# Attention beside a two-dimensional Fourier filter: the filter's steps regrouped into threes, its product copied out of the bank, a weight split moved to VectorE

## The chip, the cores and the metric

The kernel runs on one core of a Trainium2 chip. The metric is the device time of one execution in microseconds. The engines named here are TensorE (PE in the profile, its weight loads PEld), VectorE (DVE), ScalarE (ACT), GpSimd (POOL) and SyncE (SP), which only issues DMA transfers.

## The reference

Two independent halves are computed and put side by side. The first is attention with 16 query heads and one shared key and value head; the second is a filter in the frequency domain.

```python
# S, D, H, Dh = 2048, 448, 16, 28
q = (x @ wq) split into 16 heads;  k = x @ wk;  v = x @ wv
scores = einsum("bhqd,bkd->bhqk", q, k) * Dh ** -0.5
a = (softmax(scores) @ v, heads joined) @ wo

X = rfft2(xB)                       # (2048, 448) -> (2048, 225)
y = irfft2(X * (w_r + 1j * w_i))
out = concatenate([a, y], axis=-1)
```

All inputs and outputs are float32.

## The kernel before

A first part projects the queries, keys and values, prepares the keys and does the first stage of the Fourier transform (the lines up to 450). After it comes one long loop, in which the change lies.

The loop runs over 16 pairs (c, g): four chunks c of 512 queries and four groups g of four heads. For each pair it makes 16 steps, one for each 128 keys, so there are 256 steps. A step makes four score matmuls (L719), one for each head, into four PSUM banks; ScalarE takes the exponential of each (L720) into SBUF tiles p. The value products of a step (L699, eight records in the profile) follow later: `flush` issues them for all steps of the batch before, at the end of a batch. A batch is an entry of `PLAN`, a list of steps that share one such change from scores to value products and back. A step's entry names the units that it also carries. The units are small pieces of the other work: F ends the first transform; A (`fft2_a`, 16 of them) multiplies two columns by the matrix g1 in three matmuls (L484 to L486) and then by the filter on VectorE; B (`fft2_b`, 16) multiplies by g2; Z (32) is the third stage, in turn `fft3_a` and `fft3_b`, two of each for each of eight parts; W (48) is the output projection.

PAIR is two steps with no unit, THERE three steps with B in the first and A in the second, OUT three steps with two W, BACK three steps with one Z. A unit in the first step comes after that step's third score, in a later step after its fourth.

Each score and each unit takes a PSUM bank from the head of a queue, `take()`. A score's bank goes to the tail at once, a unit's bank comes back by `give(bank, n)` n scores later. There are six banks s, and the banks sx and po join them; one bank at a time holds the output being summed, so seven go round. Whoever takes a bank waits until it has been read. The orders of TensorE and VectorE are exactly those in which the program writes them; those of the other queues are set by a scheduler that keeps the dependences.

On VectorE a unit A means: the multiplies with the filter's real and imaginary part (L525 to L527, which read the bank), their sum (L528), a rounding to the matmul format (L530) and the remainder (L532); then `fft2_split` for the next A (L514, L515). A unit B means a copy of its bank to cst (L543), and each second B is followed by a store of cst to a scratch tensor t2 in DRAM (L546). At the end of a pair (c, g) its output bank is copied to osb (L707), and four `norm` calls per pair (five operations each, L606 to L613) divide it by the softmax sums; the rule `has_time(step)` says which steps may carry one. Each pair's fifth step builds the next pair's queries (`build_q`, L189 to L191 on VectorE, then nine transfers on SyncE).

`fft2_load` fetches the inputs of two A's, b on SyncE and wr and wi on GpSimd's queue. `fft3_load` fetches the inputs of four Z's: c from t2 on SyncE (L561) and constants on GpSimd's queue. The first of them needs all of t2, which means all 16 B. `wo_split` fetches a group of the output weights and splits it into a rounded part and a remainder, for the W units: a transfer and two operations on GpSimd (L478 to L480), in steps 20, 28, 36 and 44.

Of the kernel before, what the change touches and what calls it, by code (L numbers as in the profile page):

```python
# [10 lines left out]
F32 = mybir.dt.float32  # L11
# [4 lines left out]
ALU = mybir.AluOpType  # L16
# [4 lines left out]
S, D, H = 2048, 448, 16  # L21
DH = D // H
DF = D // 2 + 1
# [9 lines left out]
P_BUFS = 12  # L33


PAIR, OUT, BACK, THERE = ["", ""], ["W", "W", ""], ["Z", "", ""], ["B", "A", ""]
PLAN = ([["F"], [""]] + 4 * [PAIR] + 2 * [["A", ""]] + 6 * [THERE, THERE, PAIR] + 2 * [THERE] + 2 * [["B", ""]]
        + 8 * [OUT] + 10 * [BACK] + [PAIR]
        + 3 * [BACK] + 8 * [OUT] + 9 * [BACK] + 2 * [PAIR]
        + 3 * [BACK] + 8 * [OUT] + 7 * [BACK] + 5 * [PAIR])  # L40
TAIL = 0
WARM = 10, 10

# [2 lines left out]
def kernel(ctx: ExitStack, tc: tile.TileContext, t: dict):  # L46
    nc = tc.nc
# [4 lines left out]
    fp = ctx.enter_context(tc.tile_pool(name="fp", bufs=2))  # L52
# [15 lines left out]
    def behind(ins, other):  # L68

        tc.add_manual_dep(ins.ins, other.ins.name,  # L70
                          mybir.DependencyInfo(mybir.DependencyClass.NoSync, mybir.DependencyReason.DATA),
                          reason="order of issue")
# [136 lines left out]
    with tc.tile_pool(name="w1", bufs=1) as w1, tc.tile_pool(name="p1", bufs=6, space=PSUM) as p1:  # L209
# [37 lines left out]
        with tc.tile_pool(name="x1", bufs=2) as x1:  # L247
# [18 lines left out]
            xr, wr = {}, {}  # L266
# [192 lines left out]
    def give(bank, scores=1):  # L459

        late.append([scores, bank])
# [7 lines left out]
    ap = ctx.enter_context(tc.tile_pool(name="ap", bufs=2))  # L469
    pp = ctx.enter_context(tc.tile_pool(name="pp", bufs=P_BUFS))  # L470

    begun = []
    woh = ap.tile([128, NG, D], F32R, name="woh", bufs=1)
    wol = ap.tile([128, NG, D], F32R, name="wol", bufs=1)

    def wo_split(g):
        w = ap.tile([128, D], F32, name="wo", tag="ya")
        behind(nc.gpsimd.dma_start(w, t["wo"][:, g]), begun[-1])  # L478
        nc.gpsimd.tensor_copy(woh[:, g], w)
        nc.gpsimd.tensor_tensor(wol[:, g], w, woh[:, g].bitcast(F32), op=ALU.subtract)  # L480


    def mm3(out, w, h, l):
        mm(out, fc[w + "h"], h, start=True, stop=False)  # L484
        mm(out, fc[w + "l"], h, start=False, stop=False)  # L485
        mm(out, fc[w + "h"], l, start=False, stop=True)  # L486
# [20 lines left out]
    def halves2(bank):  # L507
        return bank[:, :2 * DF].rearrange("p (n f) -> p n f", n=2)
# [8 lines left out]
    def fft2_a(u):  # L517
        q, v = divmod(u, 2)
        s = slice(2 * v, 2 * v + 2)
        b, wr, wi = (b2[n, q][:, s] for n in ("b", "wr", "wi"))  # L520
        bank = take()
        pu = halves2(bank)
        mm3(pu, "g1", b2["h", u], b)
        pf, p2 = fp.tile([128, 2, DF], F32, name="pwr"), fp.tile([128, 2, DF], F32, name="pwi")
        nc.vector.tensor_tensor(pf, pu, wr, op=ALU.mult)  # L525
        nc.vector.tensor_tensor(p2[0:64], pu[64:128], wi[64:128], op=ALU.mult)
        nc.vector.tensor_tensor(p2[64:128], pu[0:64], wi[0:64], op=ALU.mult)  # L527
        nc.vector.scalar_tensor_tensor(pf, p2, sgn, pf, op0=ALU.mult, op1=ALU.add)  # L528
        h = fp.tile([128, 2, DF], F32R, name="ph")
        nc.vector.tensor_copy(h, pf)  # L530
        p = fp.tile([128, 2, DF], F32R, name="pl")
        nc.vector.tensor_tensor(p, pf, h.bitcast(F32), op=ALU.subtract)  # L532
        pr[u] = h, p
        give(bank, 2)

    def fft2_b(u):
        v = u % 2
# [107 lines left out]
    def at(step, f, *a):  # L645
        later.setdefault(max(step, 0), []).append((f, a))

    todo = {"F": [(fft1_b, 7)],
            "A": [(fft2_a, u) for u in range(16)],
            "B": [(fft2_b, u) for u in range(16)],  # L650
            "W": [(wo_unit, c, k, g) for c in range(NC - 1) for k in range(4) for g in range(NG)],
# [3 lines left out]
    place, where = [], {}  # L655
    for b, batch in enumerate(PLAN):
        for i, kinds in enumerate(batch):
# [10 lines left out]
        if u % 2 == 0 and u < 14:  # L668
            at(step - 1, fft2_load, u // 2 + 1)
    for g in range(NG):  # L670
        at(20 + 8 * g, wo_split, g)
    for q in range(8):
        at(max(where["Z"][4 * q] - 8, where["B"][-1] + 1), fft3_load, q)

# [1 line left out]
    norms = deque()  # L676

    def has_time(step):
        b, i, _ = place[step]
        if step % 16 == 4:  # L680
            return False
        if PLAN[b] is THERE:
            return i == 0 and len(norms) > 4
        return i < 2

    def waits_for_output(c):
        return where["W"][16 * c - 1] if c else -1
# [5 lines left out]
    def flush(b, last=False):  # L693
        while pend and pend[0][0] < b:
            _, c, g, kc, ps = pend.pop(0)
            if kc == 0:
                po[c, g] = take() if po else ps_o.tile([128, 512], F32, name="po")
            for i in range(4):
                mm(po[c, g][32 * i:32 * i + 32], vs[:, kc], ps[i // 2][:, i % 2], start=(kc == 0), stop=(kc == 15))  # L699
            if kc == 15:  # L700
                o = osb[c, g] = ap.tile([128, CW], F32, name="osb")
                if last:
                    for k in range(4):
                        s = slice(128 * k, 128 * k + 128)
                        nc.scalar.activation(o[:, s], po[c, g][:, s], AF.Copy)
                else:
                    nc.vector.tensor_copy(o, po[c, g])  # L707
                    give(po[c, g])
                    norms.extend((c, g, k) for k in range(4))

    for c, g in order:
        for kc in range(16):
            ps = []
            b, i, kinds = place[step]
            for n in range(4):
                if n % 2 == 0:
                    ps.append(pp.tile([128, 2, CW], F32, name="p"))
                sc = take()
                begun.append(mm(sc, ka[:, kc * 128:(kc + 1) * 128], qa[c, g][:, n], start=True, stop=True))  # L719
                nc.scalar.activation(ps[-1][:, n % 2], sc, AF.Exp, scale=SCALE)  # L720
                scored(sc)

                if n == (3 if i else 2):
                    for k in kinds:
                        f, *a = todo[k].popleft()
                        f(*a)
            if i + 1 == len(PLAN[b]):
                flush(b)
            if step == 1:
                give(ps_x.tile([128, 512], F32, name="sx", tag="aux"))  # L730
            pend.append((b, c, g, kc, ps))
            for f, a in later.pop(step, []):
                f(*a)
            if norms and has_time(step) and step > waits_for_output(norms[0][0]):
                norm(*norms.popleft())
            if kc == 4 and step < 240:
                build_q(*order[step // 16 + 1])
            step += 1
# [8 lines left out]
    def partial(k):  # L747
        ws.append(take()[:, :D])
        wo_mm(ws[k], c, k, range(NG - 1))

    for k in range(TAIL):
        partial(k)
    flush(len(PLAN), True)
    for k in range(TAIL, 4):
# [125 lines left out]
```

## Time and profile before

| | us |
|---|---|
| three runs | 658.11, 659.64, 659.93 (median 659.64) |
| the profiled execution | 657.37 |
| its span | 655.6 |
| TensorE busy in the span | 649.4 |
| ScalarE busy | 556.0 |
| VectorE busy | 348.9 |
| GpSimd busy | 63.3 |

The span runs from the first to the last instruction of the profiled execution. The granted TensorE clock is 1.000 throughout. The busy times are shares of one span and overlap; a busy matmul is one that has begun and is modelled not to have ended. In rows of a timeline the first number is the start and the second the length, both in microseconds, and "x16" says that 16 instructions were merged into the row. In rows of groups the last numbers are the total busy time in microseconds and the mean of one instruction in nanoseconds. In rows of DMA issues stand the size of one transfer and the median time from its issue to its landing.

The first score of the loop starts at 70.17, step 10 at 89.64. In the plan before, the A units lie in steps 10 to 66, the B units in 14 to 70, the W units in 72 to 94, 137 to 159 and 201 to 223, the Z units in 96 to 134, 161 to 198 and 225 to 243.

### The profile page before, as it was taken

Reading aid. Unit: us, or ns where it says so; the run is one execution under the profiler, and the core shown is the slowest. Engines: PE = TensorE matmul, PEld = TensorE weight load, DVE = VectorE, ACT = ScalarE, POOL = GpSimd, SP = SyncE. Lnnn points to the kernel's source line nnn. Section 1 sums busy time; section 2 is a strip of 40 time slices with the busy share of each in tenths; the row PEclk is TensorE's granted clock in tenths of the full one; section 3 lists DMA queues with packets and bytes.
Section 4 is the critical chain, followed back from the end, with each engine's and each line's share of the span. In section 5 each row is a group of like instructions: output and inputs, shape, how many; then the busy total and the mean of one; then the engine's idle time right before and its main releaser. Section 6 shows DMA issues by size and latency. Waiting matters only on the chain.

```text
span 655.6 us, 11894 instructions
## 1 busy us (share of the span) xinstructions
PE 649.4 (99%) x4480; PEld 376.5 (57%) x4480; DVE 348.9 (53%) x785; ACT 556.0 (85%) x1103; POOL 63.3 (10%) x113
## 2 busy tenths in 40 slices
PE   9999999999999999999999999999999999999997
PEld 6877545555555555565655555655555565555545
DVE  6999448778888851047371701057452502076603
ACT  5554998998888898899998988899999988899992
POOL 3022203212110000001010000000101000010100
PEclk9999999999999999999999999999999999999999
DMA  8756766736352251204141311114150303112001
GB/s 301 255 155 169 197 170 165 183 93 174 101 150 73 70 138 32 63 20 120 41 110 29 94 31 46 47 43 110 44 123 15 96 14 90 32 40 55 29 0 57
DMA packets 34250, 61.86 MB, mean 94 GB/s; under 512 B 6529, under 2 KB 22802, under 8 KB 33228
## 3 DMA queue, kind: packets, MB, share of 16 engines
q1 hardware_dynamic: 30544, 49.18, 27.1%
q0 software_dynamic: 3072, 11.00, 6.6%
q8 instruction: 36, 0.59, 0.4%
q10 hardware_dynamic: 576, 0.92, 0.4%
q14 instruction: 22, 0.18, 0.1%
HBM read 29.35 MB, written 14.75 MB: 67 GB/s over the span
## 4 chain that ended last, share of the span: by engine, by line
PE 88%; DVE 1%; ACT 0%; ACTq 0%; issue 0%; DVEq 0%
PE s L719 29%; PE s L699 29%; PE po L719 5%; PE sx L719 5%; PE sx L699 4%; PE s L619 4%; PE po L699 2%; PE s L582 2%; PE s L570 1%; PE po L619 1%; PE s L486 1%; PE s L484 1%; PE s L485 1%; PE sx L570 0%; ACT yb L624 0%; PE sx L619 0%
## 5 line engine op out<-in xcount | busy, mean ns | idle before, releaser
L720 ACT ACTIVATE p<-s 128x512 f32<-128x512 f32 x759 | 414.9, 653 | 45.1 <-PE s L719 44.3
L719 PE MATMUL s<-qa,ka 128*128 128x512 f32 x759 | 242.4, 408 | 0.6 <-ACT vs L448 0.6
L699 PE MATMUL s<-p,vs 128*32 128x512 f32 x1664 | 194.2, 596 | 0.0
L719 PEld LDWEIGHTS s<-qa,ka 128*128 128x128 f32 x759 | 137.5, 188 | 87.7 <-ACT p L720 62.8
L699 PEld LDWEIGHTS s<-p,vs 128*32 128x32 f32 x1664 | 46.6, 109 | 107.1 <-issue 103.5
L720 ACT ACTIVATE p<-sx 128x512 f32<-128x512 f32 x129 | 84.4, 654 | 6.9 <-PE sx L719 6.8
L720 ACT ACTIVATE p<-po 128x512 f32<-128x512 f32 x136 | 87.1, 641 | 3.4 <-PE po L719 3.2
L607 DVE RECIPROCAL r<-r 128x128 f32<-128x128 f32 x64 | 61.0, 953 | 2.2
L626 DVE COPY ya<-s 128x448 f32<-128x448 f32 x10 | 6.2, 625 | 101.3 <-PE s L619 101.3
L719 PE MATMUL po<-qa,ka 128*128 128x512 f32 x136 | 55.4, 407 | 0.0
L719 PE MATMUL sx<-qa,ka 128*128 128x512 f32 x129 | 52.7, 408 | 0.0
L590 POOL TENSOR_TENSOR yo<-y 128x226 f32<-128x226 f32 x16 | 9.7, 606 | 376.5 <-issue 287.9
L584 DVE COPY m<-s 128x452 f32<-128x452 f32 x13 | 8.2, 629 | 45.9 <-PE s L582 44.8
L719 PEld LDWEIGHTS sx<-qa,ka 128*128 128x128 f32 x129 | 24.2, 188 | 14.1 <-ACT p L720 9.5
L719 PEld LDWEIGHTS po<-qa,ka 128*128 128x128 f32 x136 | 25.6, 188 | 9.2 <-ACT p L720 5.0
L699 PE MATMUL sx<-p,vs 128*32 128x512 f32 x256 | 30.1, 596 | 0.0
L302 PE MATMUL pq<-xh,wqh 128*128 128x512 f32 x64 | 25.7, 401 | 0.0
L302 PE MATMUL pq<-xh,wql 128*128 128x512 f32 x64 | 25.3, 395 | 0.2
L306 ACT ACTIVATE qraw<-pq 128x512 f32<-128x512 f32 x16 | 9.2, 600 | 17.5 <-PE pq L302 17.5
L608 DVE TENSOR_TENSOR osb<-osb,r 128x128 f32<-128x128 f32 x64 | 18.8, 293 | 2.2
L606 DVE STREAM_SHUFFLE r<-osb 128x128 f32<-128x128 f32 x64 | 19.0, 297 | 0.0
L572 DVE COPY z<-s 113x512 f32<-113x512 f32 (+1 forms) x11 | 7.6, 691 | 21.3 <-PE s L570 21.3
(190 smaller groups left out, 698.5 us busy)
## 6 DMA issues: line engine op xcount, KB each, us to landing
qa<-qa SPq DMA_DIRECT2D x15, 512.0 KB, 4.3
raw<-xa SPq DMA_DIRECT2D x16, 256.0 KB, 4.8
xb<-xb SPq DMA_DIRECT2D x8, 512.0 KB, 3.6
qa<-qh SPq DMA_DIRECT2D x60, 64.0 KB, 2.0
qa<-ql SPq DMA_DIRECT2D x60, 64.0 KB, 2.0
ob<-yo SPq DMA_DIRECT2D x16, 226.0 KB, 2.2
t<-bs SPq DMA_DIRECT2D x16, 225.0 KB, 4.4
wr<-wr POOLq DMA_DIRECT2D x16, 225.0 KB, 4.8
```

The costliest lines, as they stand in the source:

```text
L302: mm(pq, w[:, j, gs], x[:, j], start=(j == 0 and n == 0), stop=(j == 3 and n == 1))
L306: nc.scalar.activation(qraw[:, g, cs], pq, AF.Copy)
L582: mm(py[:, k], z[:w, r, js], cs3[:w, k], start=True, stop=True)
L584: nc.vector.tensor_copy(m, py)
L590: nc.gpsimd.tensor_tensor(yo[:, 0:2], y1[:, 0], y1[:, 1], op=ALU.add)
L606: nc.vector.stream_shuffle(r, o, [DH] * 32)
L607: nc.vector.reciprocal(r, r)
L608: nc.vector.tensor_tensor(o, o, r, op=ALU.mult)
L619: mm(p, x[c][:, g, s], w[:, g], start=(g == 0 and n == 0), stop=(g == NG - 1 and n == 2))
L699: mm(po[c, g][32 * i:32 * i + 32], vs[:, kc], ps[i // 2][:, i % 2], start=(kc == 0), stop=(kc == 15))
L719: begun.append(mm(sc, ka[:, kc * 128:(kc + 1) * 128], qa[c, g][:, n], start=True, stop=True))
L720: nc.scalar.activation(ps[-1][:, n % 2], sc, AF.Exp, scale=SCALE)
```

## The change

Five things change in the loop.

1. The plan. In place of pairs and of threes with two units the Filter stage has two batches A, six batches BOTH (the same as THERE) and then A and B in turn, each in a batch of three with one unit. The last two A and three B come after the first eight OUT. All pairs are gone but the four at the start, and there are 88 batches instead of 94. The A units now lie in steps 10 to 67, 97 and 103, the B units in 16 to 70, 100, 106 and 109; the Z units start at 112. The rest has the same order.
2. In `fft2_a` VectorE first copies the bank to an SBUF tile us, and the multiplies read us. The bank is given back one score later instead of two.
3. `wo_split` is parted: the transfer stays on GpSimd's queue, six steps ahead, in steps 28, 34, 40 and 46; the rounding and the remainder are made on VectorE in steps 34, 40, 46 and 52, after the cst copy of a B.
4. `has_time` now says: the first two steps of any batch without an A, except each pair's fifth step. In the Filter stage the norms so start at step 34 instead of 21.
5. By the same formula as before, the first `fft3_load` now stands at step 110, as the last B is at 109; before it stood at 88.

```diff
-PAIR, OUT, BACK, THERE = ["", ""], ["W", "W", ""], ["Z", "", ""], ["B", "A", ""]
-PLAN = ([["F"], [""]] + 4 * [PAIR] + 2 * [["A", ""]] + 6 * [THERE, THERE, PAIR] + 2 * [THERE] + 2 * [["B", ""]]
-        + 8 * [OUT] + 10 * [BACK] + [PAIR]
-        + 3 * [BACK] + 8 * [OUT] + 9 * [BACK] + 2 * [PAIR]
-        + 3 * [BACK] + 8 * [OUT] + 7 * [BACK] + 5 * [PAIR])
+PAIR, OUT, BACK = ["", ""], ["W", "W", ""], ["Z", "", ""]
+A, B, BOTH = ["A", "", ""], ["B", "", ""], ["B", "A", ""]
+PLAN = ([["F"], [""]] + 4 * [PAIR] + 2 * [A] + 6 * [BOTH] + [B] + 6 * [A, B] + 8 * [OUT] + 2 * [A, B] + [B]
+        + 9 * [BACK] + 8 * [OUT] + 13 * [BACK] + 8 * [OUT] + 10 * [BACK])
...
+    def wo_load(g):
+        wo[g] = ap.tile([128, D], F32, name="wo", tag="ya")
+        behind(nc.gpsimd.dma_start(wo[g], t["wo"][:, g]), begun[-1])
+
     def wo_split(g):
-        w = ap.tile([128, D], F32, name="wo", tag="ya")
-        behind(nc.gpsimd.dma_start(w, t["wo"][:, g]), begun[-1])
-        nc.gpsimd.tensor_copy(woh[:, g], w)
-        nc.gpsimd.tensor_tensor(wol[:, g], w, woh[:, g].bitcast(F32), op=ALU.subtract)
+        nc.vector.tensor_copy(woh[:, g], wo[g])
+        nc.vector.tensor_tensor(wol[:, g], wo[g], woh[:, g].bitcast(F32), op=ALU.subtract)
...
         mm3(pu, "g1", b2["h", u], b)
+        us = fp.tile([128, 2, DF], F32, name="us", bufs=1)
+        nc.vector.tensor_copy(us, pu)
+        give(bank)
         pf, p2 = fp.tile([128, 2, DF], F32, name="pwr"), fp.tile([128, 2, DF], F32, name="pwi")
-        nc.vector.tensor_tensor(pf, pu, wr, op=ALU.mult)
-        nc.vector.tensor_tensor(p2[0:64], pu[64:128], wi[64:128], op=ALU.mult)
-        nc.vector.tensor_tensor(p2[64:128], pu[0:64], wi[0:64], op=ALU.mult)
+        nc.vector.tensor_tensor(pf, us, wr, op=ALU.mult)
+        nc.vector.tensor_tensor(p2[0:64], us[64:128], wi[64:128], op=ALU.mult)
+        nc.vector.tensor_tensor(p2[64:128], us[0:64], wi[0:64], op=ALU.mult)
...
-        give(bank, 2)
...
     for g in range(NG):
-        at(20 + 8 * g, wo_split, g)
+        at(where["B"][g + 6] - 6, wo_load, g)
+        at(where["B"][g + 6], wo_split, g)
...
-        if PLAN[b] is THERE:
-            return i == 0 and len(norms) > 4
-        return i < 2
+        return i < 2 and "A" not in PLAN[b]
```

More of the change, by code (lines that the diff above doesn't have):

```diff
@@ L474 @@
     wol = ap.tile([128, NG, D], F32R, name="wol", bufs=1)
+    wo = {}
+    def wo_load(g):
+        wo[g] = ap.tile([128, D], F32, name="wo", tag="ya")
+        behind(nc.gpsimd.dma_start(wo[g], t["wo"][:, g]), begun[-1])
     def wo_split(g):
-        w = ap.tile([128, D], F32, name="wo", tag="ya")
-        behind(nc.gpsimd.dma_start(w, t["wo"][:, g]), begun[-1])
-        nc.gpsimd.tensor_copy(woh[:, g], w)
-        nc.gpsimd.tensor_tensor(wol[:, g], w, woh[:, g].bitcast(F32), op=ALU.subtract)
+        nc.vector.tensor_copy(woh[:, g], wo[g])
+        nc.vector.tensor_tensor(wol[:, g], wo[g], woh[:, g].bitcast(F32), op=ALU.subtract)
     def mm3(out, w, h, l):
```

## The prediction

> **What bounds the kernel now.** I read the page first, then the busy time by windows, the timelines of the three engines that matter, the chain of waits, the waits of the weight loads and the DMA issues.
>
> ```profile
> PE 649.4 (99%) x4480; PEld 376.5 (57%) x4480; DVE 348.9 (53%) x785; ACT 556.0 (85%) x1103; POOL 63.3 (10%) x113
> ```
> ```profile
> 89.60:230.60 141.00, 140.71 (x844) 75.91 (x840) 116.63 (x234) 125.17 (x251) 22.68 (x38) 1.00 0.49 128
> ```
>
> TensorE has no room left. The second line is a window, with the share of each engine in turn: the Filter stage, steps 10 to 71; VectorE is busy 116.63 of 141.00 us, the fullest stretch it has, and ScalarE 125.17, that is 2.02 us a step or 6.06 for three. A busy TensorE may still be waiting, since the ends of matmuls are modelled; so I count starts, here in the five plain pairs at the end:
>
> ```profile
> 629.54 1.92 PE L699 MATMUL s<-p,vs 128*32 128x512 f32 x16
> ...
> 632.44 0.39 PE L719 MATMUL sx<-qa,ka 128*128 128x512 f32 x1
> 632.67 0.86 PE L719 MATMUL s<-qa,ka 128*128 128x512 f32 x3
> 633.47 1.92 PE L699 MATMUL s<-p,vs 128*32 128x512 f32 x16
> ```
>
> Scores start 0.233 us apart (632.44 to 632.67, and 0.86 less 0.39 over two). The second fence comes from the chain:
>
> ```profile
> 97.80 1.85 PE po L699 x16
> ...
> 103.87 1.85 PE po L699 x16
> ...
> 110.39 1.85 PE po L699 x16
> ...
> 115.32 2.71 PE s L699 x24
> ...
> 205.04 2.71 PE s L699 x24
> ```
>
> Sixteen value products take 1.85 and twenty-four 2.71, so a step's eight cost 0.86. A plain pair lasts 3.93 (629.54 to 633.47); less 8 x 0.233 and 2 x 0.86 that leaves 0.35, paid once a batch for going from scores to value products and back. From 97.80 to 103.87 lies a batch of three with two units that empties a pair: 6.07 = 1.72 + 2.80 + 0.35 + two units, so a unit is 0.6. This builds every batch: three steps with one unit after three steps 2.80 + 2.58 + 0.35 + 0.6 = 6.33, with two units 6.93, both above ScalarE's 6.06. TensorE stays the bound, and only two things move the end: the number of batches, and waits in which TensorE stands still.
>
> **What is taken away.** The plan goes from 94 batches to 88 with the same scores, value products and units: 6 x 0.35 = 2.1 us off.
>
> The old waits of the Filter stage go too. The batch from 103.87 has the same make as the one before and lasts 6.52: 0.45 lost. From 110.39 to 115.32 is 4.93 where the build gives 4.79: 0.15. From 115.32 to 205.04 lie five rounds of two threes with two units and a pair, 89.72; one round builds to 17.78, so 0.8 is lost. The waits of the weight loads name one more:
>
> ```profile
> PEld sx L484 <- DVE bh L514: 0.7, 1, 0.7
> ```
>
> That is the second unit A, at step 12; with the other half of its operand behind it I put 0.8. Together 2.2 us, which I take off whole and put back below where they return. The output weights' split leaves GpSimd; its four loads of them stay on GpSimd's queue, two batches ahead of their use, behind loads of wr and wi whose buffers are free by then. Those two batches, 12.7 us, hide them; if the queue held them up longer, VectorE would stand at the split and the copies behind it would be late.
>
> **What is added: VectorE's work and its order.** TensorE waits when VectorE reads a product's bank too late. Seven banks go round. A unit in the first step (after three scores) has its product about 1.6 us after the batch's first score, and its bank is asked for again at the last step's third score: 0.1 + 10 x 0.233 + 0.6 = 3.0 us. In a batch with two units it is the second score, 3.4 us. VectorE's prices:
>
> ```profile
> 121.42 0.63 DVE L525 TENSOR_TENSOR pwr<-s,wr 128x450 f32<-128x450 f32 x1 [1.14 <-PE s L486]
> ...
> 126.05 0.62 DVE L543 COPY cst<-s 128x450 f32<-128x450 f32 x1
> ```
> ```profile
> 222.84 0.54 DVE L189 TENSOR_SCALAR qt<-qraw,mask,cvec 128x512 f32<-128x512 f32 x1
> ...
> 224.49 0.01 DVE L606 LOAD_MASK_SELECT r<-osb  x1
> ...
> 228.31 0.01 DVE L606 LOAD_MASK_SELECT r<-osb  x1
> ...
> 230.43 0.01 DVE L606 LOAD_MASK_SELECT r<-osb  x1
> ```
> ```profile
> L515 DVE TENSOR_TENSOR b<-b,bh 128x450 fp32r<-128x450 f32 x16 | 10.0, 628 | 0.6
> ...
> L707 DVE COPY osb<-s 128x512 f32<-128x512 f32 x12 | 8.3, 689 | 18.2 <-PE s L699 18.2
> L526 DVE TENSOR_TENSOR pwi<-s,wi 64x450 f32<-64x450 f32 x13 | 8.2, 629 | 0.4
> ```
>
> A unit A with the next split takes 4.63 (121.42 to 126.05), building queries 1.65 (222.84 to 224.49), a norm 2.12 (228.31 to 230.43), a product's copy 0.62 (L543), an eviction of an output bank about 0.6. The new copy is the cst copy by shape and source, with its start 0.66; its bounds are nothing and the 0.69 of L707. The multiplies then read SBUF: two inputs from SBUF cost 628 ns (L515), one from PSUM 629 (L526), so nothing is gained there, and A becomes 5.29. [...] A group of output weights costs VectorE a subtraction of 0.63 (L515) and a cast between nothing and 0.69; I take 1.0.
>
> With these, place by place:
> - Second A, now at step 13: TensorE comes 0.94 later (a step more in the batch before), its operand 0.66 later, so of the 0.8 stay 0.4.
> - Step 20: the eviction of the first output bank meets a batch with two units, 0.2, as it did in pairs.
> - Steps 20 to 24: with t from the first score of step 19, the product of A at 20 is there at 3.5, VectorE is done at 8.8, builds queries until 10.4 and only then copies B's product of step 22, until 11.05. That bank is asked for at 6.93 + 0.1 + 3.4 = 10.4: 0.6, and 0.1 for restarting the weight load. 0.7.
> - Steps 34 to 39: with t from step 34, VectorE comes free from A at 32 at 1.8; cst to 2.4, output weights to 3.4, two norms to 7.6, eviction 8.2, queries 9.8, and the copy for A at 37 ends at 10.5. Its bank is asked for at 6.33 + 3.0 = 9.3. 1.3 with the restart.
> - Steps 226 to 231: a copy and two sums, two norms, eviction, queries, then the copy of the next product at about 10.4; asked for at 9.9. 0.5. Before, the norms fell on 225, 226 and 229, with one less ahead of this copy.
> - The pairs of batches from 40 to 67: 0.6 + 1.0 + 2 x 2.12 from 1.6 ends at 7.4, the next A's product comes at 7.9. Hidden, with half a microsecond and the 0.8 that the bank allows.
>
> **What is added: the third transform right behind the second.** Before, the last B was at step 70 and the first Z at 96. Now they stand at 109 and 112, one batch apart. SyncE's issues before:
>
> ```profile
> 229.51 0.53 SPq L546 DMA_DIRECT2D t<-cst  x1
> 230.98 0.50 SPq L201 DMA_DIRECT2D qa<-qa  x1
> 232.23 2.80 SPq L561 DMA_DIRECT2D c<-t  x4
> 240.79 0.36 SPq L628 DMA_DIRECT2D oa<-ya  x1
> 241.20 1.87 SPq L561 DMA_DIRECT2D c<-t  x4
> ```
> ```profile
> t<-bs SPq DMA_DIRECT2D x16, 225.0 KB, 4.4
> ...
> c<-t SPq DMA_DIRECT2D x32, 112.5 KB, 2.5
> ```
>
> The first load waits for the last store, 229.51 to 232.23 = 2.72; four loads take 1.87 to issue, the last begins after three quarters of it, 1.40; a load lands after 2.5. With t from step 109: product 1.6, copy to 2.3, store, first load 5.0, last load 6.4, landed 8.9. The first Z wants it at 6.33 + 0.8 = 7.1. TensorE stands for 1.9 with the restart, and behind it in its order all scores, so ScalarE too. Behind the waiting loads on SyncE stand the next loads of this kind and the queries of step 116, due at 128; they have time. On GpSimd the Z's constants are fetched well ahead. The bounds: 1.2 if the store lands in the 2.5 of a load and the four issues take half a microsecond less, and 4.5 if the issue is the slow one above (2.80 for 1.87) and the store takes the 4.4 of the first transform's stores (first line of the last fence).
>
> **The sum.** 0.4 + 0.2 + 0.7 + 1.3 + 0.5 + 1.9 = 5.0 added, 2.1 + 2.2 = 4.3 taken away: 0.7 slower. The profiled execution took 657.37 (span 655.6 and 1.8 around it), so 658.1; that execution lies 2.27 below the median of the runs, 659.64, and against the median the forecast is 660.3. About 0.3%, 2 us, is what a measurement of this kernel can tell from no change.
>
> **The rivals.**
> - The third transform's load is later than I have it, slower: all four transfers, the store ahead of them and the wait of TensorE lie in one chain, and each microsecond there is a microsecond of the end. A wait of 4.1 instead of 1.9 gives 662.5; it decides from a wait of 3.3 on. For it: the slow issue and the 4.4 us stores. Against: at 230.98 the slow one shared its queue with a transfer of queries that is not there at step 110. Chance 0.15.
> - VectorE's backlog grows, slower: if its operations in this stage come out 6% longer, each chain of eight to ten microseconds ahead of a bank is half a microsecond longer, in four places, and an eviction joins them: about 2.4 more than the forecast, 662.7; it decides from 1.3 on. For it: 116.63 of 141.00 already, and no plain pairs left to catch up in. Against: the work is spread over 48 more steps, and GpSimd's arithmetic beside it is gone. Chance 0.17.
> - The new waits hardly come, faster: VectorE runs further ahead than I have it and the load lands sooner, as in its lower bound. With 1.5 left of 5.0 the end is 656.8. For it: each of the four waits is the small difference of two long sums. Against: two have over a microsecond. Chance 0.12.
> - ScalarE becomes the bound in the batches of three with one unit: 6.06 against 6.33, no.
>
> **How the numbers follow.** The forecast, between 2 us faster and 2 us slower, has 0.56. Faster by over 0.3% is the third rival, 0.12; slower the first two, 0.32. The range goes from 657.2, a little into the faster case, to 663.6, where both slower rivals with their bounds are mostly in.
>
> **What would show it.** After: 88 runs of value products; a round of A and B batches 12.66 us apart without gaps; a wait of the first Z's weight load on the DMA of c of about 1.9; scores at steps 24 and 39 waiting for VectorE's cst and us copies by 0.6 and 1.2; a wait for m at 231. If the first Z waits for nothing, or VectorE's waits appear at every A, the sum is wrong. If batches without waits last other than 6.33 and 6.93, the base of it all is.

## The result, and the profile after

The changed kernel takes 661.72 us in the median of its first 8 runs (660.33 to 664.16), the kernel before 659.24 beside it on the same chip (8 runs): a ratio of 1.0043, with a 95% interval of 1.0031 to 1.0054. In a second set of 12 runs it is 1.0029 [1.0013, 1.0044]. It is slower, by 2.48 us in the first set and 1.92 in the second; forecast were 0.7.

The page of the changed kernel, busy times and the shares of the chain that ended last:

```profile
PE 649.5 (98%) x4480; PEld 378.7 (57%) x4480; DVE 359.4 (54%) x809; ACT 556.6 (84%) x1103; POOL 55.4 (8%) x105
...
PE 83%; DVE 3%; DMA 1%; issue 1%; ACT 0%; SPq 0%; ACTq 0%; DVEq 0%
```

VectorE has 10.5 us more, GpSimd 7.9 less, and the chain, which before had 88% on TensorE, 1% on VectorE and nothing on a DMA, now passes 3% through VectorE and 1% through a DMA: those are the new waits. How long a batch is that waits for nothing is seen in the chain, in steps 40 to 66 (value products of whole batches: start, length):

```profile
165.57 2.71 PE s L703 x24
171.87 2.71 PE s L703 x24
178.19 2.71 PE s L703 x24
...
203.46 2.71 PE po L703 x24
209.78 2.71 PE po L703 x24
216.12 2.71 PE po L703 x24
```

A batch with A and one with B take 6.30 and 6.32, as built (6.33). So the batches without a wait are those of the forecast, and each batch can be held against its build: its length from its first score to the next batch's, less 0.2325 a score, 0.857 for each step of value products, 0.345 for the change there and back, 0.613 a unit (0.88 a Z), which are the forecast's prices to one digit more. What is left over is lost to waits. All losses from step 10 on, in microseconds:

| first step of the batch | forecast | changed | kernel before |
|---|---|---|---|
| 10 | 0 | 0.42 | 0 |
| 13 (before: 12) | 0.4 | 0.42 | 0.80 |
| 19 (forecast for step 20; before: 17 and 20) | 0.2 | 0.33 | 0.44 and 0.16 |
| 22 | 0.7 | 0.80 | 0 |
| 37 (before: 36, 52, 57) | 1.3 | 1.22 | 3 x 0.26 |
| 112, the first Z | 1.9 | 2.51 | 0 |
| 229 | 0.5 | 0.59 | 0 |
| all batches (those not listed come to -0.51 and +0.25) | 5.0 | 5.78 | 2.43 |

From the start of step 10 to the end of the span the changed kernel takes 566.88 and the kernel before 565.95: 0.93 more, of which the forecast had 0.7. The waits of the weight loads name the causes; here the windows 118 to 128, 152 to 164, 316 to 324 and 580 to 592, one line of each:

```profile
PEld s L723 <- DVE cst L548: 1.0, 1, 1.0
...
PEld s L723 <- DVE us L528: 1.3, 1, 1.3
...
PE s L575 <- DMA c<-t: 2.3, 1, 2.3
...
PEld s L723 <- DVE m L589: 0.8, 1, 0.8
```

The timelines of SyncE and TensorE at the first Z (start, length, and in brackets the idle time before):

```profile
314.33 0.33 SPq L551 DMA_DIRECT2D t<-cst  x1
317.38 3.65 SPq L566 DMA_DIRECT2D c<-t  x8
```
```profile
318.31 0.50 PE L723 MATMUL po<-qa,ka 128*128 128x512 f32 x1
318.64 0.63 PE L723 MATMUL s<-qa,ka 128*128 128x512 f32 x2
321.57 1.10 PE L575 MATMUL s<-fi,c 128*113 128x128 f32 x8 [2.30 <-DMA c<-t]
```

The last store is issued at 314.33, the first dependent load 3.05 later (forecast 2.72), the Z 4.19 after that (forecast 1.40 + 2.5 = 3.9). After three scores TensorE stands for 2.30. Eight loads stand in the row and not four: those of the next four Z's follow at once. The chain that ended last goes through the fourth, from 318.70, which is 1.32 after the first; so the issue was as forecast, and the landing, 2.7 to 2.9, slower than the 2.5.

That leaves 1.0 to 1.5 us of the medians. They lie in two places that the forecast held constant. First, the device time is more than the span: by 1.73 to 1.87 in every run of the kernel before, by 2.20 to 2.31 in every run of the changed one, which is 0.48 more on the mean. Second, the clock. The profiled execution took 661.85 (span 659.6), and its step 10 begins 3.05 later than in the earlier profile. Half of that is the loop's first step, which lasts 3.65 instead of 2.13; the cause is in this row of the windows (the third figure from the end is the granted clock):

```profile
72.00:74.00 2.00, 2.00 (x15) 0.99 (x18) 1.55 (x2) 1.90 (x4) 2.00 (x4) 0.50 0.93 230
```

TensorE runs at half clock for 3.41 us from 71.81, at the loop's first step. The other half is the start-up: the loop's first score begins at 71.68 instead of 70.17, and over the fourteen profiles of this study, whatever the kernel, it begins between 70.17 and 73.60. Whether the half clock belongs to the change is the first thing to test.

### The profile page after: what moved, and what is told of

The parts are those of the page before. It is cut to its first block, busy times and chain, and to the rows that moved or that the text cites. A ratio compares the mean times of both kernels' runs of the same rounds, so it can differ in the third digit from the quotient of the medians.

```text
span 659.6 us, 11909 instructions
## 1 busy us (share of the span) xinstructions
PE 649.5 (98%) x4480; PEld 378.7 (57%) x4480; DVE 359.4 (54%) x809; ACT 556.6 (84%) x1103; POOL 55.4 (8%) x105
## 4 chain that ended last, share of the span: by engine, by line
PE 83%; DVE 3%; DMA 1%; issue 1%; ACT 0%; SPq 0%; ACTq 0%; DVEq 0%
PE s L723 29%; PE s L703 21%; PE po L703 6%; PE sx L703 6%; PE sx L723 4%; PE po L723 3%; PE s L624 3%; PE po L624 3%; PE s L575 2%; PE s L587 1%; PE s L489 1%; PE s L488 1%; PE s L487 1%; DVE r L612 1%; DMA t<-cst 0%
## 5 line engine op out<-in xcount | busy, mean ns | idle before, releaser
L724 ACT ACTIVATE p<-s 128x512 f32<-128x512 f32 x807 | 433.7, 660 | 46.4 <-PE s L723 46.0
L723 PE MATMUL s<-qa,ka 128*128 128x512 f32 x807 | 252.5, 408 | 2.4 <-DVE us L528 1.0
L703 PE MATMUL s<-p,vs 128*32 128x512 f32 x1280 | 148.6, 596 | 0.0
L703 PEld LDWEIGHTS s<-p,vs 128*32 128x32 f32 x1280 | 36.3, 109 | 82.8 <-issue 79.6
L724 ACT ACTIVATE p<-po 128x512 f32<-128x512 f32 x98 | 62.4, 637 | 1.8 <-PE po L723 1.8
L703 PE MATMUL po<-p,vs 128*32 128x512 f32 x384 | 45.3, 597 | 0.0
L703 PE MATMUL sx<-p,vs 128*32 128x512 f32 x384 | 44.9, 596 | 0.0
L723 PE MATMUL po<-qa,ka 128*128 128x512 f32 x98 | 39.6, 404 | 0.1
L703 PEld LDWEIGHTS sx<-p,vs 128*32 128x32 f32 x384 | 10.8, 109 | 24.8 <-issue 24.5
L703 PEld LDWEIGHTS po<-p,vs 128*32 128x32 f32 x384 | 10.5, 109 | 23.3 <-issue 22.2
```

## The experiments

Twelve runs follow, two of them of a kernel without an edit. "Step 10 to the end" is taken from each one's profile, as above, and stands against 565.95 for the kernel before and 566.88 for the changed one. The clock lost in a set is the mean over its runs of (1 - mean granted clock) x span; the clock is on record to 0.001, which is 0.66 us in a single run.

**The kernel before, once more.** No edit.

> The kernel before, unchanged, to see the time before the loop. In the profile after, TensorE's clock was granted at half for 3.41 us around the first step, step 10 began 3.05 us later than in the profile before, and from step 10 to the end the two differ by 0.95 us only, while the medians differ by 2.5. Theory S (chance of the start): the half clock strikes the kernel before as well; most of its runs show a mean clock near 0.997 and only the profile shown before escaped it; then the medians' difference has to come from the loop or from another part. Theory C (the change does it): its runs show 1.000, step 10 begins near 89.6 in its profile, and about 1.5 us of the 2.5 is this half clock.

Measured: 659.72 against 659.14, 1.0004 [0.9991, 1.0017]; 565.89 from step 10 to the end, and in its profile the windows at the loop's start:

```profile
72.00:74.00 2.00, 2.00 (x15) 1.06 (x18) 1.65 (x2) 1.96 (x4) 2.00 (x4) 0.58 0.95 226
74.00:76.00 2.00, 2.00 (x12) 1.12 (x5) 1.26 (x3) 0.53 (x2) 0.09 (x1) 0.56 0.99 250
```

The same 3.41 us at half clock, from 72.33, in the old kernel. It is chance and common to both: of this set's ten runs six have a mean clock of 0.997 (660.03 on the mean) and four 1.000 (658.69). Step 10 starts at 92.72, as late as in the changed kernel's profile (92.69). The first profile of the kernel before was one without it, and with the earliest first score of all (70.17; here 71.81).

**The third transform away from the second.** The last B comes six steps ahead of the first Z instead of three; a bare batch stands between, and one A and one B share a batch in its place.

```diff
-8 * [OUT] + 2 * [A, B] + [B]
+8 * [OUT] + [A, BOTH, B, B, BARE]        # BARE = ["", "", ""]
```

> The changed kernel with the last two A and three B as A, BOTH, B, B and a batch with no unit, so that the last B is at step 106, six steps ahead of the first Z, in the same 88 batches. Theory W (the first Z's wait on the chain store, load is a wait of its own): the 2.51 us lost in the batch of step 112 goes, ScalarE bounds the bare batch by some 0.3, and the time falls by 2.2 us against the changed kernel: a ratio to the kernel before of about 1.001 where the change had 1.0043. Rival (the wait would only pass to the next loads or to VectorE): the batches from 112 to 130 lose as much in another place and the ratio stays at 1.004.

Measured: 659.45, 1.0002 [0.9992, 1.0012]; 565.02 from step 10 to the end, 1.86 less than the changed kernel. TensorE and SyncE there:

```profile
318.60 0.50 PE L723 MATMUL s<-qa,ka 128*128 128x512 f32 x1
318.94 0.39 PE L723 MATMUL po<-qa,ka 128*128 128x512 f32 x1
319.17 0.40 PE L723 MATMUL s<-qa,ka 128*128 128x512 f32 x1
319.40 1.03 PE L575 MATMUL s<-fi,c 128*113 128x128 f32 x8
```
```profile
308.35 0.33 SPq L551 DMA_DIRECT2D t<-cst  x1
310.87 3.65 SPq L566 DMA_DIRECT2D c<-t  x8
```

The load is issued 2.52 after the store and is down long before the Z at 319.40, which follows its score without a gap. The loss of 2.51 is gone; the bare batch loses 0.58, since it builds to 5.70 and takes 6.28: there ScalarE, with 6.06 of exponentials for three steps, takes longer than the build. All other losses stay. The wait at the first Z is so shown to be the largest single cost of the change.

**No norm before step 37.**

```diff
-        return i < 2 and "A" not in PLAN[b]
+        return i < 2 and "A" not in PLAN[b] and step > 36
```

> The changed kernel with no norm before step 37, so the two norms of steps 34 and 35 come later. Theory W (the wait at step 39 is VectorE's row of norms and queries ahead of A's copy): the 1.22 us lost in the batch of step 37 goes to under 0.1, nothing else in the Filter stage grows, the first Z still loses 2.5: ratio 1.0025. Rival (VectorE is simply full in this stage): the loss comes back in the batches from 40 to 72 and the ratio stays at 1.004.

Measured: 660.60, 1.0018 [1.0005, 1.0031]. The loss at 37 is gone and none has grown for it elsewhere: the chain that the prediction added up there (output weights, two norms, eviction, queries, copy) is right, and the norms are the part that can go. But at the first Z 4.07 were lost, not 2.51, and step 10 to the end came to 567.28. The windows show why:

```profile
318.00:320.00 2.00, 0.07 (x1) 0.10 (x2) 0.00 (x0) 0.82 (x2) 0.00 (x0) 1.00 0.92 234
320.00:322.00 2.00, 2.00 (x10) 1.90 (x11) 0.25 (x1) 0.00 (x0) 0.00 (x0) 0.57 0.45 102
322.00:324.00 2.00, 2.00 (x7) 1.57 (x6) 1.91 (x5) 1.89 (x4) 0.00 (x0) 0.58 0.00 0
```

TensorE waits 2.26 there for the loads, and then gets half its clock for 3.41 us, from 320.27. I had not expected that; the changed kernel once more (below) is the test of it.

**Without the copy.** The multiplies read the bank, which is given back two scores later, as before the change.

```diff
-        us = fp.tile([128, 2, DF], F32, name="us", bufs=1)
-        nc.vector.tensor_copy(us, pu)
-        give(bank)
+        us = pu
...
+        give(bank, 2)
```

> The changed kernel without the copy of A's product: the multiplies read the bank, and it goes back two scores later as in the kernel before. Theory W (the copy is paid by giving the bank back): VectorE has 0.66 us less for each A, but a bank in a batch with one unit is read 1.97 us long where some 1.4 to 1.6 are hidden: 0.3 to 0.4 lost in each batch with an A alone, ten of them, about 2 in the one of step 37, together some 3 us slower than the changed kernel: ratio 1.009. Rival (the copy is VectorE work for nothing): VectorE's rows get shorter, the waits at steps 22 and 39 shrink by 0.6 each, and the ratio falls to 1.0025.

Measured: 667.56, 1.0125 [1.0106, 1.0143]; 574.66 from step 10 to the end. Each of the six batches with one A that the changed kernel passes without a loss now loses 0.43 to 0.49, and the one at step 37 loses 3.85 (half clock from 158.46 included). The first A loses 1.34, and the first Z 3.90, with half clock from 325.71. The waits in the window 152 to 163:

```profile
PEld s L722 <- DVE pwi L531: 2.0, 1, 2.0
PE s L722 <- DVE pwi L531: 1.7, 1, 1.7
```

A score waits for the third multiply, the last reader of the bank. So the copy pays for itself in this plan, by giving the bank back two operations earlier: some 6 us of the medians (8.42 over the kernel before, against 2.48 and 1.92), twice what I had expected. From step 10 to the end the traces differ by 7.78, but some 3 of that are the two spells of half clock.

**The copy alone,** in the kernel before, with its plan and its split.

```diff
+        us = fp.tile([128, 2, DF], F32, name="us", bufs=1)
+        nc.vector.tensor_copy(us, pu)
+        give(bank)
-        nc.vector.tensor_tensor(pf, pu, wr, op=ALU.mult)
+        nc.vector.tensor_tensor(pf, us, wr, op=ALU.mult)
...
-        give(bank, 2)
```

> The kernel before with the copy of A's product alone (and its bank given back one score later instead of two); plan and split as before. VectorE gets 0.66 us more for each of 16 A. Theory W (in two threes and a pair VectorE has the room): only the second A at step 12 waits 0.66 longer, 1.4 lost instead of 0.8, the other losses of the Filter stage stay at 0.2 to 0.5 each: ratio 1.001. Rival (VectorE has no room for the copy in any plan): 0.3 to 0.6 more is lost in each round of eight steps: ratio 1.004.

Measured: 662.23, 1.0047 [1.0029, 1.0065]: my expectation missed, the rival's 1.004 was right. Each of the six losses of the old plan grew by 0.63 to 0.69, the length of one copy; 0.37 at step 10 are new. At steps 12 and 17 TensorE waits for the next A's operand bh, 1.1 and 0.6. At steps 20, 36 and 52 it is this, of the waits in the window 90 to 230:

```profile
PEld sx L721 <- DVE osb L709: 1.1, 1, 1.1
PEld s L721 <- DVE osb L709: 1.1, 1, 1.1
PEld po L721 <- DVE osb L709: 1.0, 1, 1.0
```

The eviction of an output bank stands in VectorE's order behind an A. In the old plan it is already late by 0.2 there, so what is put ahead of it on VectorE goes straight to the end.

**The split alone,** in the kernel before.

```diff
-        at(20 + 8 * g, wo_split, g)
+        at(where["B"][2 * g + 4] - 6, wo_load, g)
+        at(where["B"][2 * g + 4], wo_split, g)      # both operations on nc.vector
```

> The kernel before with the split of the output weights on VectorE alone, after the B's of steps 30, 38, 46 and 54, loads six steps ahead; plan and the rest as before. Theory W (the split costs VectorE about 1 us a time and takes GpSimd's arithmetic away from VectorE's side): the 0.44 lost in the batch of step 17, beside GpSimd's first split, goes, nothing is added, since the rounds have a plain pair each: ratio 0.9995. Rival (VectorE pays for it in waits): 0.5 lost at each split: ratio 1.003.

Measured: 660.14, 1.0017 [1.0004, 1.0029]; 566.60 from step 10 to the end. Between my expectation and the rival's. The loss at 17 (0.44) is gone, but the batch at 57 loses 1.21 instead of 0.26; 0.36 at step 10 and 0.16 more at step 20 are new, and their cause stays open. VectorE and TensorE there:

```profile
193.37 0.38 DVE L483 CAST woh<-wo 128x448 fp32r<-128x448 f32 x1
193.78 0.63 DVE L484 TENSOR_TENSOR wol<-wo,woh 128x448 fp32r<-128x448 f32 x1
194.34 0.01 DVE L610 LOAD_MASK_SELECT r<-osb  x1
...
200.12 0.39 DVE L518 CAST bh<-b 128x450 fp32r<-128x450 f32 x1
```
```profile
200.65 0.44 PE L488 MATMUL s<-bh,g1h 128*128 128x450 f32 x1 [0.66 <-DVE bh L518]
```

The split takes 0.97 (193.37 to 194.34), and the operand of the next A, seven microseconds on, is late by as much: it starts 2.89 after the batch's first score (197.23), in the kernel before 1.93 (197.65 after 195.72). GpSimd's loads of the output weights came early enough in both places.

**Gap, and the queries one step earlier.** On top of the gap, `build_q` goes from each pair's fifth step to its fourth, away from the copy that waited behind it at steps 24 and 39.

```diff
-        if step % 16 == 4:          # has_time: no norm in this step
+        if step % 16 == 3:
...
-            if kc == 4 and step < 240:
+            if kc == 3 and step < 240:
```

> The changed kernel with the last B six steps ahead of the first Z, as in the run with the gap, and with the queries built after each pair's fourth step instead of the fifth, norms not there. Theory W (the waits at 22, 39 and 231 are queries that fall between an A or two norms and the next copy): these three, 2.6 us together, go and 0.5 comes at one A near step 54; the loop from step 10 takes 563 us against 565.9 before: ratio 0.997. Rival (VectorE is full and the waits move): the sum of losses stays near 3.9 and the ratio at 1.000.

Measured: 657.12 against 659.34, 0.9970 [0.9956, 0.9984], as expected, and 563.11 from step 10 to the end: faster than both kernels. The losses at 22, 37 and 229 (2.6 in all) are gone; 0.65 at step 52 and 0.18 at step 100 are new. At 52 it is the same pile in another place:

```profile
185.53 0.68 DVE L711 COPY osb<-s 128x512 f32<-128x512 f32 x1
186.13 0.54 DVE L188 TENSOR_SCALAR qt<-qraw,mask,cvec 128x512 f32<-128x512 f32 x1
...
187.78 0.62 DVE L548 COPY cst<-s 128x450 f32<-128x450 f32 x1
```

**Late Z.** The first Z stands in the third step of its batch, with no gap.

```diff
+LATE = ["", "", "Z"]
-        + 9 * [BACK] + 8 * [OUT]
+        + [LATE] + 8 * [BACK] + 8 * [OUT]
```

> The changed kernel with the first Z in the third step of its batch instead of the first, the last B left where it is; no bare batch. The wait for the loads should shrink from 2.5 to 0.6. Theory W with the clock (a wait of over 2 us of TensorE is at times followed by 3.41 us at half clock, which costs 1.6 more): with 0.6 no half clock follows near 318 us, the runs' mean clock lies at 0.997 to 1.000 as in the kernel before, and the ratio falls to 1.001. Rival (the half clock comes by chance anywhere): runs with 0.994 to 0.996 stay as frequent as in the changed kernel, and the ratio is 1.002 to 1.003.

Measured: 659.54, 1.0002 [0.9991, 1.0013]; 565.44 from step 10 to the end. The batch loses 0.82 instead of 2.51, and here the Z waits for nothing:

```profile
320.86 1.67 PE L723 MATMUL s<-qa,ka 128*128 128x512 f32 x4
322.53 1.13 PE L575 MATMUL sx<-fi,c 128*113 128x128 f32 x8
```

What is left is ScalarE (the four scores before take 1.67, not 1.09). So two edits that do nothing but keep TensorE from standing at the first Z each give back 1.4 to 1.9 us in the trace, and bring the ratio from 1.0029 or 1.0043 to 1.0002.

**The split back on GpSimd,** in the changed kernel, at the same steps.

```diff
-        nc.vector.tensor_copy(woh[:, g], wo[g])
-        nc.vector.tensor_tensor(wol[:, g], wo[g], woh[:, g].bitcast(F32), op=ALU.subtract)
+        nc.gpsimd.tensor_copy(woh[:, g], wo[g])
+        nc.gpsimd.tensor_tensor(wol[:, g], wo[g], woh[:, g].bitcast(F32), op=ALU.subtract)
```

> The changed kernel with the split of the output weights back on GpSimd, in the same steps; all else as changed. Theory W (the split's 1.0 us on VectorE stands in the row ahead of A's copy at step 37): the loss there falls from 1.22 to 0.2 to 0.3, the first Z still waits 2.5: about 0.9 us faster than the changed kernel. Rival (GpSimd's subtraction stretches a VectorE operation beside it by the 0.8 that the profile before shows): the gain is lost again at steps 40 to 52, and the time is that of the changed kernel.

Measured: 660.26, 1.0021 [1.0006, 1.0036], which the runs can't tell from the changed kernel's 1.0029. In the profile I was wrong: the batches from 31 to 37 lose 3.4 us instead of 1.2, and step 10 to the end takes 568.87, though the first Z loses 1.81 and not 2.51. GpSimd and VectorE there:

```profile
146.72 1.42 POOL L483 TENSOR_TENSOR wol<-wo,woh 128x448 fp32r<-128x448 f32 x1
...
153.85 1.15 POOL L483 TENSOR_TENSOR wol<-wo,woh 128x448 fp32r<-128x448 f32 x1
```
```profile
147.05 1.34 DVE L517 CAST bh<-b 128x450 fp32r<-128x450 f32 x1
...
153.28 0.57 DVE L617 CAST oh<-osb 128x128 fp32r<-128x128 f32 x1
153.88 1.27 DVE L618 TENSOR_TENSOR ol<-osb,oh 128x128 fp32r<-128x128 f32 x1
```

A rounding that takes 0.39 alone takes 1.34 beside GpSimd's subtraction, a subtraction of 0.29 takes 1.27. At these two splits VectorE's operations beside GpSimd's rounding and subtraction took 1.5 and 1.3 longer in all, more than the 0.97 that had been taken off VectorE. The runs do not bear out all of this loss: by the profile (with the time around the span and the clock) they should be 1.3 us slower than the changed kernel's of the same set, and they are 0.39 faster.

**The changed kernel, once more.** No edit.

> The changed kernel itself once more, to count the runs by their mean clock. Theory W with the clock (the first Z's wait is at times followed by 3.41 us at half clock): a third or more of the runs at 0.994 to 0.996, which neither the kernel before nor the run with the gap has, and the ratio near 1.003 to 1.004. Rival (chance of the first eight runs): clocks spread as in the kernel before, 0.997 to 1.000, and the ratio near 1.0015.

Measured: 660.65 against 658.73, 1.0029 [1.0013, 1.0044], 12 runs. This time the profile has no half clock at the loop's start, but this at the first Z (timeline of TensorE; windows):

```profile
319.99 2.02 PE L575 MATMUL s<-fi,c 128*113 128x128 f32 x8 [2.67 <-DMA c<-t]
321.66 0.78 PE L723 MATMUL s<-qa,ka 128*128 128x512 f32 x1
```
```profile
316.40:319.60 3.20, 0.92 (x7) 0.45 (x3) 0.20 (x1) 1.73 (x4) 0.00 (x0) 1.00 0.76 200
319.60:323.00 3.40, 3.01 (x11) 2.85 (x12) 0.88 (x3) 0.53 (x2) 0.00 (x0) 0.50 0.38 83
```

Eight matmuls of the Z take 2.02 instead of 1.10: half clock, for 3.41 us from 319.62. The batch loses 4.32, all others are as in the first profile. Of five profiles in which the Z waits (the changed kernel twice, no norms, no copy, split on GpSimd) three have half clock right behind the wait (waits of 2.67, 2.26 and 2.09 us), two have not (2.30 and 1.60): the length alone doesn't decide. Of the five with the gap or the late Z, in which it doesn't wait, none has. The runs without a trace agree as far as they go. One spell gives a mean clock of 0.997 (the first profile of the changed kernel), two gave 0.994 (no early norms); so 0.996 or lower asks for more than the one at the loop's start. It occurs in 2 of the 94 runs of the kernel before that stood beside the experiments, in 16 of 46 runs of the kernels in which the Z waits (5 of 20 of the changed one), and in 3 of 51 with the gap or the late Z. In this set it was 2 of 12, where I had expected a third or more.

**One operation of the split on each engine.** On the version with gap and early queries, first only the rounding goes back to GpSimd, then only the remainder. In question was what lies around the span.

```diff
-        nc.vector.tensor_copy(woh[:, g], wo[g])        # the first kernel
+        nc.gpsimd.tensor_copy(woh[:, g], wo[g])
```
```diff
-        nc.vector.tensor_tensor(wol[:, g], wo[g], woh[:, g].bitcast(F32), op=ALU.subtract)   # the second
+        nc.gpsimd.tensor_tensor(wol[:, g], wo[g], woh[:, g].bitcast(F32), op=ALU.subtract)
```

> Base: the version with the gap before the third transform and the queries one step earlier; of the split only the rounding of a group goes back to GpSimd, the remainder stays on VectorE. In question is the time that lies around the profile's span: 1.78 to 1.82 us in the four kernels so far whose split is on GpSimd, 2.23 to 2.61 in the seven with the split on VectorE, 2.33 in the base. Theory K (it hangs on GpSimd having a rounding to make in the loop): 1.8 here. Theory C (it hangs on how many instructions GpSimd has, 174 or more against 170): 1.8 here too. Theory V (it hangs on VectorE having part of the split): 2.3 here. In the loop VectorE loses four operations of 0.38 and may wait for GpSimd's, from step 10 to the end between 562.8 and 563.8 (base 563.11). Ratio 0.9965 by K or C, 0.997 by V.

> The same base; of the split only the remainder goes back to GpSimd, the rounding stays on VectorE. Time around the span: 2.3 by theory K (no rounding on GpSimd), 1.8 by theory C (four instructions more on GpSimd), 2.3 by theory V. In the loop GpSimd's subtraction of 1.15 to 1.42 us stretches what VectorE does beside it, as in the kernel with the whole split on GpSimd, where batches 31 to 37 lost 2.2 us more than in the changed kernel: here 0.5 to 2 us over the base, 563.6 to 565.1 from step 10 to the end. Ratio 0.998 to 1.000.

Measured: 657.67, 0.9960 [0.9945, 0.9975] and 656.94, 0.9956 [0.9943, 0.9968]; the second is the lowest time of the study, and the intervals of the three versions overlap. Around the span lie 1.83 to 1.90 in the first and 2.07 to 2.16 in the second. The first rules out that it hangs on VectorE having a part of the split, the second that it hangs on the number of GpSimd's instructions alone (174 here, and the kernels with 1.8 to 1.9 have 173 to 175). That it hangs on GpSimd's roundings fits best, but 2.13 here, 2.26 in the changed kernel, 2.33 in the base and 2.61 in the version with only the gap have none in the loop alike. What sets this time stays open; over the runs of one program it keeps within 0.1 of its mean.

In the loop the first took 564.56 (expected 562.8 to 563.8), for the most part because its batches at 10 and 13, ahead of any split, lost 0.8 more than the base's. The second missed on the good side: 563.48 from step 10 to the end (expected 563.6 to 565.1), no batch from 31 to 37 loses anything. GpSimd's subtraction now waits for VectorE's rounding, and so falls beside the norm behind it:

```profile
149.65 1.15 POOL L483 TENSOR_TENSOR wol<-wo,woh 128x448 fp32r<-128x448 f32 x1 [15.04 <-DVE woh L482]
```
```profile
149.49 0.30 DVE L611 STREAM_SHUFFLE r<-osb 128x128 f32<-128x128 f32 x1
149.82 0.95 DVE L612 RECIPROCAL r<-r 128x128 f32<-128x128 f32 x1
```

Both keep their usual 0.30 and 0.95.

## Why the prediction came out as it did

- **The base held.** 88 batches, 6.33 and 6.93 long where nothing waits; six changes at 0.35 saved; the old waits gone where it said. TensorE stayed the bound.
- **Five of the new waits held** within 0.13: those at 13, 19, 22, 37 and 229 came to 3.36 where 3.1 were forecast. Taking away the norms removed the wait at 37, moving the queries removed those at 22, 37 and 229, so the causes of these three are shown, not only their sizes; those at 13 and 19 are argued. The 0.1 for restarting the weight load is in the trace of before: of the second A's matmuls the two that waited (L484 at 95.50, L486 at 96.16) took 0.47, the one between them 0.37.
- **Not in the sum: the first batch of three, 0.42 at step 10.** It comes after a pair and builds to 2.80 + 1.72 + 0.35 + 0.6 = 5.47, less than ScalarE's 6.06. The rival "ScalarE becomes the bound" was turned down for batches that follow a three (6.33) and not looked at for the one that follows a pair; three score loads of this batch do wait for ScalarE's p in the trace (0.30, 0.30 and 0.19), but it takes 5.88 and not 6.06, and no kernel tested the reading.
- **Mis-sized: the wait at the first Z.** 1.9 forecast, 2.51 and 4.32 lost in the two profiles of the changed kernel. Store to load took 3.05 and 3.48 there (forecast 2.72, from a single row of before), and the first load to the Z 4.19 and 4.13 (3.9). This is the first rival, "the load is later than I have it"; 2.51 is a quarter of the way to its 4.1. Its limit of 3.3 is passed only where half clock follows the wait: what a batch loses beyond its wait is 0.21 in the two profiles without it and 1.65 to 1.81 in the three with it, so a spell costs 1.4 to 1.6 us, in part of the runs. The prediction did not have this at all: it priced standing still at the time stood.
- **Wrong as a constant: the time around the span.** "Span 655.6 and 1.8 around it" became 2.26 with this change.
- **In part luck: the loop's 0.93 so near to 0.7.** The waits came to 0.78 more than forecast; against that the old waits, which went, were 0.23 more than forecast, and from the last batch to the end of the span the changed kernel is 0.35 quicker, against the kernel before, than the builds say, which no term had. By the prediction's own limits the 2.48 of the first set falls to the case of more than 2 us slower, which it gave 0.32, and the 1.92 of the second just to the forecast's; the range holds both.
- **The median added up.** In the second set: 0.93 in the loop, 0.48 around the span and 1.43 - 0.97 = 0.46 of clock lost make 1.87; measured 1.92. (0.93 is from the profile without half clock in the loop, so that the clock is not counted twice.) In the first set: 0.93 + 0.48 + (2.14 - 0.92) = 2.63; measured 2.48. The 0.92 is the mean over the 94 runs of the kernel before. Three others with the wait gone fit as well: with the gap -0.93 + 0.83 + 0.52 = 0.42 (measured 0.31), with the late Z -0.51 + 0.48 + 0.07 = 0.04 (measured 0.20), with gap and early queries -2.84 + 0.55 - 0.02 = -2.31 (measured -2.22). The copy alone does not: 3.52 + 0.02 + 0.57 = 4.1, measured 2.89; nor does the split back on GpSimd: 2.92 + 0.04 + 0.28 = 3.2, measured 1.53. Their profiles lost more than their runs.
- **The copy.** Its price (0.66 to A, nothing gained by the multiplies) held. The second of the multiplies, by its line in the changed kernel and in the kernel before (least, median and greatest of a group, in ns):

```profile
L532 DVE TENSOR_TENSOR pwi<-us,wi x16: 623/624/625, 95.7 to 302.4; 64x450 f32<-64x450 f32 x16
```
```profile
L526 DVE TENSOR_TENSOR pwi<-s,wi x13: 628/629/631, 103.7 to 217.9; 64x450 f32<-64x450 f32 x13
```

  All three take 628, 624 and 622 ns from SBUF against 627, 629 and 621 from the bank, so SBUF as the source gained at most 5 ns an operation. Not seen in the prediction: that the copy is what lets batches with one A pass without a loss, and that in the old plan it costs 2.9.
- **The split.** A group costs VectorE 0.97 (forecast 1.0) and the queue order did not hurt, as forecast. That GpSimd's arithmetic beside VectorE is a cost was only a half-sentence of a rival; the split back on GpSimd shows up to 1 us for each operation that meets it.

## What to carry to other kernels

When the bound engine is full, price an edit of the order by the room ahead of each wait, place by place: the same copy costs 0.65 us at each wait that has no room ahead of it (the six of the old plan), and saves some 6 us in all where it frees a bank in time. A dependence through DRAM between two stages (store, load, use: 6.5 to 7.6 us in the five profiles where the use waited) needs that much other work between them in the plan, and of the four waits of TensorE between 2.1 and 2.7 us three were followed by half clock here, which cost 1.4 to 1.6 more. Before comparing a single profile with another, run the old kernel again: the three microseconds that the change seemed to cost at the start were in the old kernel's second profile too.

## What the chip showed that was not expected

TensorE's clock fell to half for 3.41 us at a time. In the first trace of the changed kernel it did so from 71.81 to 75.22 (3.413 us in the trace's clock record), and the next change came 583.68 us later, 171 times 3.413; the two spells of the kernel without the copy, from 158.46 and from 325.71, begin 49 times 3.413 apart. The changes in these traces so lie on a grid, and where a wait falls on it would decide whether it costs extra, which no run tested, but which fits that a wait of 2.09 us was followed by it and one of 2.30 was not. The traces bear this out at the first Z: in the grid's stretch of 3.41 us that holds most of the wait TensorE was busy 1.12, 1.15 and 1.32 where half clock came next, 1.70 and 1.97 where it did not; the wait of 2.30 (319.27 to 321.57) lies across a line of the grid at 320.98. Busy time alone is not the whole rule: at step 37 of the kernel without the copy half clock came after a stretch with 1.72, and at the loop's start, with 0.3 to 0.6 of idle time in the stretch, it came in four of the fourteen profiles. So waits of 2.09, 2.26 and 2.67 us, shorter than one such stretch, here cost 1.4 to 1.6 us more.

VectorE slowed down beside GpSimd by what exactly met: with the split back on GpSimd 0.39 became 1.34 and 0.29 became 1.27 where a rounding or a subtraction of two SBUF operands met GpSimd's subtraction, and in the kernel before a subtraction of 0.63 (L532, at 106.40) became 1.46, while with only the remainder on GpSimd a shuffle (0.30) and a reciprocal (0.95) beside it kept their time. What sets the two kinds apart no run tested.
